# Batch 0 of a fused attention and mixer kernel: first loads in five pieces on one queue, casts on ScalarE, two buffer fills on GpSimd

## The chip, the cores and the metric

The kernel runs on one core of one Trainium2 chip. A core has a matrix engine (TensorE, PE in the profile; its weight loads are PEld), VectorE (DVE), ScalarE (ACT), GpSimd (POOL) and SyncE (SP), each with its own instruction queue that it works through in order, and 16 DMA engines. DMAs are issued from queues: SP and ACT have hardware queues (q1 and q10 in this profile), POOL has a software queue (q0). In this kernel the loads from POOL's queue turn float32 into bfloat16 on the way, the others do not.

The metric is the device time of one execution in microseconds (us). Four executions took 293.96 to 294.33 us, median 294.16 us. Times inside an execution are counted from the start of the profiled span.

## The reference

```python
B, H, S, D = 8, 8, 576, 64                      # q, k, v: [B, H, S, D] float32
scores = (q @ k.transpose(0, 1, 3, 2)) / sqrt(D)
scores = where(pos[:, None] // 64 >= pos[None, :] // 64, scores, -1e9)   # causal in blocks of 64
attn = softmax(scores)
x = (attn @ v).transpose(0, 2, 1, 3).reshape(B, S, 512)
xt = x.transpose(0, 2, 1)
h = relu(xt @ w_tok1) @ w_tok2                  # over the 576 tokens, 256 hidden
u = x + h.transpose(0, 2, 1)
out = u + relu(u @ w_ch1) @ w_ch2               # over the 512 channels, 1536 hidden
```

The row maximum is not subtracted in the kernel: it exponentiates the scores as they are and divides by the row sums.

## The kernel before

**Stages of a batch.** For each half of the heads ("hg", 0 or 1, four heads each) q and k are loaded, brought to bfloat16 and transposed in 32x32 blocks on DVE (line 440, tile `turned`). Scores are made transposed, keys on partitions and queries on columns (line 555, PSUM tiles `sc`). ACT exponentiates them into `e_sb` (line 574, 1024 columns at a time: 512 columns of two heads). DVE zeroes the 64x64 corners that the block mask excludes (line 580). PE multiplies by `vals`, which is v with a column of ones (line 602), so that the row sum comes out as the 65th column; DVE takes the reciprocal (line 624) and scales (line 630) into `x_sb`. Then come the token mixing (lines 788, 817, 832 and, from batch 1 on, 881), the channel products up (line 999) and down (line 1319, from batch 1 on 1228), and the output DMAs.

**Columns of e_sb.** Keys 0 to 511 are four blocks J of 128. The scores of a head are kept in 1536 columns, `ECOL[J]` being the first column of block J: 0, 576, 1024, 1344. `SETS` says which (column, first key, first query, width) regions are made together, 512 columns a set: set 0 is J = 0 and queries 0 to 511, set 1 the rest of J = 0 and J = 1, set 2 J = 2 and 3. `MASKS` gives the columns at which a set is masked: (0), (576), (1024, 1344). The last 64 keys go their own way, into `et_sb`, a part of the tile `vals` (lines 652 and 669).

**Batch 0** has its own form (`first_attention`, line 674). Its heads go in four pairs j; for each pair the sets are made in the order 2, 1, 0, so set 0 and its mask come last. The products with `vals` of a pair depend on all exps and masks of that pair.

**First loads (`load_qk`, line 404).** Only for batch 0 and hg 0, q and k are loaded in float32 by the hardware queues into `stage` (the tile `gT`), each in two halves of 9 of the 18 tokens that a partition holds: one half issued on SP and one on ACT (line 427). Each half is then cast (line 400; planned for ACT or DVE, all four were put on ACT), and each half transposed. Everything else is loaded by software DMAs from POOL: v of batch 0 (line 469, ten pieces), k and q of hg 1 (line 420), the token weights (line 488), the channel weights (lines 511, 520), and from batch 1 on q, k and v. POOL's queue also makes the identity matrix (`masks.py`) before its first load. The plan lets at most eight of its DMAs be outstanding.

**Fills (`init_tiles`, line 339).** DVE zeroes or sets paddings at the start (line 343): first `zeros`, from which PE runs, then parts of `turned`, `e_sb`, the weights and `vals`, among them the two buffers `et_sb` (128x640 bfloat16 each; 128x320 uint32 in the profile).

**Matmuls without use (`raise_clock`, line 366).** 16 products of `zeros` (line 372) and up to 110 smaller ones (line 379) keep PE running so that its clock is up. The latter are only put where the plan sees PE free, and only up to planned time 20; their results are not used.

**The order** of every queue comes from a planner in the file (class `Plan`). It knows for each piece of work its engines, a cost in us, its dependencies, a priority, a class `urgent`, and buffers that it takes and gives. It fills each engine in planned time (`run`), tries 1000 random changes of the priorities within +-4000 and keeps those that do not make the planned end later (`search`); the instructions are then emitted in planned order. Planned times are the planner's own, they are not measured. Of software DMAs it supposes that the first starts moving data at 6.2 (`soft` in line 115) and that they then follow one another; of hardware DMAs that they follow one another from 0.7 after the first issue (`hard`, `FIRST`); a DMA's data can be used 1.3 later.

Of the kernel before, what the change touches and what calls it, by code (L numbers as in the profile page):

```python
# [31 lines left out]
class Plan:  # L32
# [66 lines left out]
    def run(self):  # L99
# [12 lines left out]
        heapq.heapify(queued)  # L112

        avail = {e: [] for e in self.LAG}
        t, hard, soft, gives, order, mode = 0.0, 0.0, 6.2, [], [], 0
        left = len(self.ops)
        landed = [0.0] * 8

# [2 lines left out]
        while left:  # L121
# [13 lines left out]
            for e in ("PE", "ACT", "DVE", "POOL", "SP"):  # L135
                if busy[e] > t or e == "POOL" and landed[-8] > t:
                    continue
                for at, a in enumerate(avail[e]):
                    if self.fits(a[3]):
                        break  # L140
                else:
                    continue
                o = a[3]
                soon = t + 0.6 * o.cost[e]
                if any(
                    r < soon and self.ops[n].urgent > o.urgent and e in self.ops[n].engines
                    for r, n in queued
                ):
                    continue
                if any(  # L150
                    -u[0] > o.urgent and self.fits(u[3], [name for r, name, _ in gives if r < soon])
                    for u in avail[e][:at]
                ):
                    continue
                for x in o.engines:
                    del avail[x][bisect.bisect_left(avail[x], o.key)]
                left -= 1
                began = True
                for pools, note in o.take:
                    note["pool"] = next(p for p in pools if self.free[p])  # L160
                    note["slot"] = self.free[note["pool"]].pop(0)
                o.engine, o.start = e, t
                o.end = busy[e] = t + o.cost[e]
                if o.mode is None:
                    o.mode = mode
                if e == "PE" and o.mode != mode:
                    o.end = busy[e] = o.end + 0.1
                    mode = o.mode
                order.append(o)
                lag = self.LAG[e]  # L170
                if o.xfer is not None:
                    first = o.end + self.FIRST[e]
                    if e == "POOL":
                        soft = max(soft, hard, first) + o.xfer
                    else:
                        hard = max(hard, first) + o.xfer
                    o.end, lag = (soft if e == "POOL" else hard), 1.3
                    if e == "POOL":
                        landed.append(o.end + lag)
                for note in o.give:  # L180
                    heapq.heappush(gives, (o.end + lag * (not o.quick), note["pool"], note["slot"]))
                for u in o.users:
                    same = u.engines == (e,) and o.xfer is None
                    u.ready = max(u.ready, o.end + (0.05 if same else lag))
                    u.waiting -= 1
                    if not u.waiting:
                        heapq.heappush(queued, (u.ready, u.n))
# [8 lines left out]
def kernel(  # L196
# [133 lines left out]
    def act_cost(n):  # L330
        return 0.08 + n * 0.000833
# [7 lines left out]
    def init_tiles():  # L339
        def fill(engine, key, prio, *parts):  # L340
            for t, value in parts:
                def emit(o, t=t, value=value):
                    (nc.vector if engine == "DVE" else nc.gpsimd).memset(t, value)

                pads.setdefault(key, []).append(P.add(engine, 0.17, emit, (), prio))

        for i, t in enumerate(kT):
            fill("DVE", ("kT", i), -1e4 + i, (t[:, S:640, :], 0.0))
        for i in range(2):
            fill(  # L350
                "DVE", ("v", i), -60 + 20 * i,
                (v1[i][64:128, 4, :, :], 0.0),
                (v1[i][:, 0:4, :, 64:65], 1.0),
                (v1[i][0:64, 4, :, 64:65], 1.0),
            )
            fill("DVE", ("e", i), -70, (e_sb[i][:, :, 1536:1600], 0.0))
            fill("DVE", ("et", i), -70, (et_sb[i], 0.0))
        fill("DVE", "zeros", -1e5, (zeros, 0.0))
        fill("DVE", "w1", -70, (w1_sb[64:128, 4, :], 0.0), (w1o_sb[0:64, :], 0.0))

        def emit(o):
            make_identity(nc, ident)

        pads["ident"] = [P.add("POOL", 0.6, emit, (), -1e6)]
# [24 lines left out]
    def warm_up():  # L389
        def emit(o):  # L390
            nc.scalar.activation(warm, nc.const_aps.tensor(0.0, (128, 1), FP32), EXP)

        P.add("ACT", 1.5, emit, (), -9e3)


    EVAC = ("DVE", "ACT")
# [7 lines left out]
    def load_qk(b, hg, after=[]):  # L404
        i = (2 * b + hg) % 3
        first = b == 0 and hg == 0
        prio = 10 * b + 4 * hg - (100 if b == 0 else 0)
        parts = ((0, NB // 2), (NB // 2, NB))
        done = []
        for n, (src, raw, dst) in enumerate(((k, kraw[i], kT[i]), (q, qraw[i], qT[i]))):  # L410
            hbm = src[b, 4 * hg : 4 * hg + 4].rearrange("h (p k) d -> (h p) (k d)", p=32)
# [6 lines left out]
            if not first:  # L418
# [1 line left out]
                    nc.gpsimd.dma_start(out=raw2, in_=hbm)  # L420

                loads = [P.add("POOL", 0.55, emit_load, raw_war, prio + n, xfer=8 * 0.184)]
            for f, (k0, k1) in enumerate(parts):
                if first:
                    def emit_load(o, k0=k0, k1=k1, hbm=hbm, st=st):
                        queue = nc.sync if o.engine == "SP" else nc.scalar
                        queue.dma_start(out=st[:, D * k0 : D * k1], in_=hbm[:, D * k0 : D * k1])

                    ld = P.add(("SP", "ACT")[f % 2], 0.45, emit_load, (), -1e4 + n, xfer=(k1 - k0) * 0.1)

                    def emit_cast(o, k0=k0, k1=k1, raw2=raw2, st=st):
                        cast(o, raw2[:, D * k0 : D * k1], st[:, D * k0 : D * k1])

                    w = D * (k1 - k0)
                    ld = P.add(EVAC, {"ACT": act_cost(w), "DVE": dve_cost(w)}, emit_cast, [ld], -1e4 + 2 + n)
                    reads(("g", 0), ld)
                    loads = [ld]

# [133 lines left out]
    def exp(dst, n, op, note, prio, urgent=0, give=None):  # L572
        def emit(o):
            nc.scalar.activation(dst, sc[SC.index(note["pool"])][:, :, 0:n], EXP, scale=scale)  # L574

        return P.add("ACT", act_cost(2 * n), emit, [op], prio, give=give or [note], urgent=urgent)

    def mask(e, c, hs, deps, prio, urgent=0):
        def emit(o):
            nc.vector.memset(e[64:128, hs, c : c + 64], 0.0)  # L580

        return P.add("DVE", 0.17, emit, deps, prio, urgent=urgent)

    def head_out(b, head, deps, prio, tail, urgent=0):
        hg, h = divmod(head, 4)

        ei = hg if b == 0 else b % 2
        vt, xt, et, e = v1[b % 2], x_sb[b % 3], et_sb[ei], e_sb[hg]
        shift = 0 if b % 2 == 0 else -64
        bank = {}  # L590

        def emit(o, chunks):
            u = bank_of(bank)[:, 0:330].rearrange("p (i c) -> p i c", c=66)
            for I in chunks:
                for J in range(I + 1):
                    if J < 4:
                        c = ECOL[J] + 128 * (I - J) + (shift if I == 4 else 0)
                        w = e[:, h, c : c + 128]
                    else:
                        c = 64 + 128 * h + (64 * hg if b else 0) + shift  # L600
# [39 lines left out]

    TAIL = (512, 512, 64)
    MASKS = ((0,), (576,), (1024, 1344))

    def first_tail(hg, heads, deps, prio):

# [28 lines left out]
    def first_attention(ready, v_ready):  # L674
# [3 lines left out]
        for j in range(4):  # L678
# [4 lines left out]
            prio = -3000 + j  # L683
            exps = []
            for n, s in enumerate((2, 1, 0)):
                width = sum(w for _, _, _, w in SETS[s])
                parts = tuple((hg,) + r for r in SETS[s])
                dst = e[:, hs, 512 * s : 512 * s + width]
                if j == 0 and n == 0:

                    note = {}
# [18 lines left out]
                if n == (1 if j else 2):  # L710
                    tails = first_tail(hg, heads, [op] + ready[hg], prio + 0.1 * n + 0.05)
                exps += these
                for c in MASKS[s]:
                    exps.append(mask(e, c, hs, these, prio, urgent=1))
            for h in heads:
                deps = exps + v_ready[hg] + pad + pads["e", hg]
# [751 lines left out]
```

## Time and profile before

| what | us |
|---|---|
| median of 4 executions | 294.16 |
| the profiled execution | 294.33 |
| its span | 292.5 |
| PE busy | 286.0 (98%) |
| DVE busy | 235.9 (81%) |
| ACT busy | 166.7 (57%) |
| POOL busy | 62.0 (21%) |
| first scores (line 555) begin | 8.51 |
| first exp (line 574) begins | 9.18 |
| last exp of batch 0 ends | 21.28 |
| first scores of batch 1 begin | 26.76 |
| last matmul group's end | 288.66 |

The profiled execution is 294.33 us long, of which the span from the first to the last profiled instruction is 292.5; 1.8 us lie around it. It stands 0.17 us above the median. PE counts as busy also while it multiplies zeros and while a matmul waits in the pipeline, so its 98% is no measure of use in the first 20 us.

### The profile page before, as it was taken

What the parts mean: (1) busy time and instruction counts of PE and PEld (TensorE: products, weight loads), DVE (VectorE), ACT (ScalarE), POOL (GpSimd) and SP (SyncE); (2) the same over time, 40 slices, a digit from 0 to 9 for tenths busy, and PEclk for the clock granted to TensorE, in tenths of its full rate; (3) what the DMA queues carried; (4) which work ended last, traced back from release to release, by engine and by line L of the source; (5) the groups of instructions that cost most, each with busy time, mean ns of one, the idle gap of its engine ahead of it and who ended that gap; (6) DMA issues with size and microseconds to landing.
All of it is one profiled execution on the core that took longest, in us unless ns stands there. A gap on an engine that the chain in (4) does not pass through costs nothing.

```text
span 292.5 us, 7674 instructions
## 1 busy us (share of the span) xinstructions
PE 286.0 (98%) x3252; PEld 180.4 (62%) x3252; DVE 235.9 (81%) x512; ACT 166.7 (57%) x236; POOL 62.0 (21%) x96
## 2 busy tenths in 40 slices
PE   8899999999999999999999999999999999999994
PEld 4566445554558765455774657775446885566883
DVE  5566768988959979959997979668998968969993
ACT  4797864576777563786656796433477004867000
POOL 8776353810430170170032000000000000000000
PEclk9999999999999999999999999999999999999998
DMA  8999999992793299995329012042000912130054
GB/s 213 187 199 210 207 186 182 225 198 81 115 131 74 43 163 198 167 129 64 73 16 211 5 32 42 2 145 54 3 0 10 154 72 74 36 142 5 0 183 145
DMA packets 64403, 31.99 MB, mean 109 GB/s; under 512 B 53104, under 2 KB 55024, under 8 KB 64368
## 3 DMA queue, kind: packets, MB, share of 16 engines
q0 software_dynamic: 44320, 17.34, 50.3%
q1 hardware_dynamic: 19760, 13.57, 17.3%
q8 instruction: 25, 0.41, 0.6%
q10 hardware_dynamic: 288, 0.59, 0.5%
q14 instruction: 10, 0.08, 0.1%
HBM read 35.85 MB, written 9.44 MB: 155 GB/s over the span
## 4 chain that ended last, share of the span: by engine, by line
PE 90%; ACT 4%; DMA 2%; DVE 1%; issue 0%; ACTq 0%
PE mm L1228 18%; PE mm L999 15%; PE sc L555 9%; PE mm L602 9%; PE mm L1319 7%; PE mm L1104 6%; PE late L1104 6%; PE mm L788 6%; PE late L1228 4%; PE mm L881 4%; ACT e_sb L574 4%; PE mm L1026 3%; DMA gT<-in_q_dram 2%; DVE turned L440 1%; PE mm L912 1%; PE mm L962 0%
## 5 line engine op out<-in xcount | busy, mean ns | idle before, releaser
L574 ACT ACTIVATE e_sb<-sc 128x1024 bf16<-128x1024 f32 x95 | 92.5, 1030 | 32.9 <-PE sc L555 32.4
L999 PE MATMUL mm<-uT,wc_sb 128*128 128x512 bf16 x192 | 46.1, 382 | 0.0
L469 POOL DMA_DIRECT2D vals<-in_v_dram x45 | 36.9, 837 | 26.3 <-PE mm L602 22.4
L440 DVE STREAM_TRANSPOSE turned<-raws 128x288 int32<-128x288 int32 x64 | 40.0, 706 | 2.2 <-ACT raws L400 1.8
L555 PE MATMUL sc<-turned 32*128 32x64 bf16 (+4 forms) x744 | 35.4, 281 | 1.4 <-DVE turned L440 0.8
L602 PEld LDWEIGHTS <-e_sb 128*128 128x128 bf16 x896 | 31.3, 97 | 6.7 <-issue 3.2
L999 PEld LDWEIGHTS <-wc_sb 128*128 128x128 bf16 x192 | 20.0, 116 | 20.8 <-issue 5.7
L602 PE MATMUL mm<-vals,e_sb 128*128 128x65 bf16 x868 | 32.5, 193 | 0.0
L630 DVE TENSOR_TENSOR x_sb<-mm,rinv 128x320 bf16<-128x320 f32 x62 | 29.1, 485 | 1.3
L776 DVE TENSOR_SCALAR gT<-mm 128x512 bf16<-128x512 f32 x27 | 18.6, 689 | 11.8 <-PE mm L999 11.7
L1228 PEld LDWEIGHTS <-sums 128*128 128x128 bf16 x252 | 24.1, 98 | 4.4 <-issue 1.2
L1228 PEld LDWEIGHTS <-gT 128*128 128x128 bf16 x240 | 22.8, 98 | 4.5 <-issue 1.3
L555 PEld LDWEIGHTS <-turned 32*128 32x128 bf16 x752 | 12.8, 93 | 19.6 <-issue 17.3
L400 ACT COPY e_sb<-mm 128x512 f32<-128x512 f32 x14 | 8.2, 591 | 26.6 <-PE mm L1104 25.0
L774 ACT ACTIVATE gT<-mm 128x512 bf16<-128x512 f32 x24 | 14.3, 597 | 10.9 <-PE mm L999 10.8
L580 DVE MEMSET e_sb<- 64x128 uint32 (+1 forms) x72 | 10.6, 153 | 10.4 <-ACT e_sb L574 6.4
L788 PE MATMUL mm<-x_sb,w_sb 128*128 128x512 bf16 (+1 forms) x102 | 17.9, 316 | 0.0
L420 POOL DMA_DIRECT2D raws<-in_k_dram x15 | 8.2, 553 | 41.3 <-DVE turned L440 32.1
L896 DVE TENSOR_TENSOR u_sb<-mm,x_sb 128x512 bf16<-128x512 f32 x24 | 15.4, 684 | 1.4 <-PE mm L881 1.3
L1251 DVE TENSOR_TENSOR o_sb<-mm,u_sb 128x512 f32<-128x512 f32 x20 | 13.7, 687 | 3.4 <-PE mm L1228 2.6
L1228 PE MATMUL mm<-wd_sb,sums 128*128 128x256 bf16 x132 | 15.7, 273 | 0.0
L1251 DVE TENSOR_TENSOR o_sb<-mm,o_sb 128x512 f32<-128x512 f32 (+1 forms) x19 | 12.0, 632 | 4.4 <-PE mm L1228 4.2
(146 smaller groups left out, 457.9 us busy)
## 6 DMA issues: line engine op xcount, KB each, us to landing
out_dram<-o_sb SPq DMA_DIRECT2D x14, 512.0 KB, 3.1
raws<-in_k_dram POOLq DMA_DIRECT2D x15, 288.0 KB, 6.3
raws<-in_q_dram POOLq DMA_DIRECT2D x15, 288.0 KB, 7.1
vals<-in_v_dram POOLq DMA_DIRECT2D x28, 128.0 KB, 5.9
wc_sb<-in_moe_w_ch_dram POOLq DMA_DIRECT2D x8, 192.0 KB, 6.5
wc_sb<-in_moe_w_ch_dram POOLq DMA_DIRECT2D x3, 512.0 KB, 10.5
out_dram<-o_sb SPq DMA_DIRECT2D x10, 128.0 KB, 2.3
vals<-in_v_dram POOLq DMA_DIRECT2D x15, 64.0 KB, 5.4
```

The costliest lines, as they stand in the source:

```text
L440: nc.vector.transpose(dst[:, 0:S, :] .rearrange("p s e -> p (s e)") .bitcast(I32) .rearrange("p (a k) -> p k a", k=NB)[:, k0:k1], raw2.bit ...
L469: nc.gpsimd.dma_start(out=dst, in_=src)
L555: nc.tensor.matmul(out=home(n)[:, c0 : c0 + w], lhsT=kT[i][r, j0 : j0 + 128, par], rhs=qT[i][r, i0 : i0 + w, par], start=(par == 0), stop= ...
L574: nc.scalar.activation(dst, sc[SC.index(note["pool"])][:, :, 0:n], EXP, scale=scale)
L602: nc.tensor.matmul(out=u[:, I, 0:65], lhsT=w, rhs=vt[:, J, head, 0:65], start=(J == 0), stop=(J == I),)
L630: nc.vector.tensor_tensor(out=xt[:, :, 64 * head : 64 * head + 64], in0=u[:, :, 0:64], in1=ri.to_broadcast([128, 5, 64]), op=MULT,)
L788: nc.tensor.matmul(out=bank_of(bank)[:, w * n : w * n + w], lhsT=wt[:, tt : tt + 255 : 2], rhs=xt[:, c, cols], start=(c == 0), stop=(c == 4),)
L999: nc.tensor.matmul(out=bank_of(bank), lhsT=wc1_sb[:, m, channels(cc)], rhs=uT[b % 2][:, :, m, :], start=(m == 0), stop=(m == NDM - 1),)
L1104: nc.tensor.matmul(out=bank_of(bank), lhsT=x(m), rhs=y[:, :, m, :], start=first and m == 0, stop=m == 1, skip_group_check=not first,)
L1228: nc.tensor.matmul(out=bank_of(bank)[:, 256 * i : 256 * i + 256], lhsT=x[:, kk, 128 * i : 128 * i + 128], rhs=y[:, kk], start=first and i ...
L1251: nc.vector.tensor_tensor(out=dst, in0=src, in1=other, op=ADD)
L1319: nc.tensor.matmul(out=ps, lhsT=gt[:, cc, c0 : c0 + 128], rhs=wc2_sb[:, cc, cols], start=(cc == 0 and not turned), stop=(cc == NDC - 1),)
```

## The change

Seven edits, all for the start of the kernel or in the planner's figures:

- `load_qk`: the first k is loaded in two pieces and the first q in three (9, 5 and 4 of the 18 tokens of a partition), all five issued on SP; none on ACT. Casts are given to ACT alone, with the highest class of urgency. The transposes of q follow the three pieces.
- `init_tiles`: the two `et_sb` buffers are zeroed on POOL, with a priority just behind the identity matrix, so ahead of POOL's loads.
- `LAST_SETS`, `LAST_COLS`, `LAST_MASKS`, `ECOL_LAST`: for batch 0, hg 1, the columns of `e_sb` are laid out anew. J = 1 takes columns 0 to 447 and J = 0 columns 448 to 1023, so both corners to be masked (columns 0 and 448) are in set 1, and set 0, the last one made, has no mask.
- the table load on ACT (`warm_up`) gets a planned time from 0.75.
- planner figures: software DMAs start at 5.0 instead of 6.2; no 0.05 between two dependent pieces on PE; an exp costs 0.02 less; an urgent mask 0.12 instead of 0.17; a hardware load costs 0.42 of issue instead of 0.45, 0.089 a token instead of 0.1, and begins at 0.7.

Because the planner sees other numbers, the order of the instructions can differ anywhere in the program. The number of useful matmuls, of exps and of masks is the same.

```diff
-        t, hard, soft, gives, order, mode = 0.0, 0.0, 6.2, [], [], 0
+        t, hard, soft, gives, order, mode = 0.0, 0.0, 5.0, [], [], 0
...
-                    u.ready = max(u.ready, o.end + (0.05 if same else lag))
+                    u.ready = max(u.ready, o.end + ((e != "PE") * 0.05 if same else lag))
...
-            fill("DVE", ("et", i), -70, (et_sb[i], 0.0))
+            fill("POOL", ("et", i), -1e5, (et_sb[i], 0.0))
...
-        P.add("ACT", 1.5, emit, (), -9e3)
+        P.add("ACT", 1.5, emit, (), -9e3, at=0.75)
...
-        parts = ((0, NB // 2), (NB // 2, NB))
...
-            for f, (k0, k1) in enumerate(parts):
+            edges = (0, 9, 18) if not (first and n) else (0, 9, 14, 18)
+            for f, (k0, k1) in enumerate(zip(edges, edges[1:])):
                 if first:
                     def emit_load(o, k0=k0, k1=k1, hbm=hbm, st=st):
-                        queue = nc.sync if o.engine == "SP" else nc.scalar
-                        queue.dma_start(out=st[:, D * k0 : D * k1], in_=hbm[:, D * k0 : D * k1])
-
-                    ld = P.add(("SP", "ACT")[f % 2], 0.45, emit_load, (), -1e4 + n, xfer=(k1 - k0) * 0.1)
+                        nc.sync.dma_start(out=st[:, D * k0 : D * k1], in_=hbm[:, D * k0 : D * k1])
+
+                    ld = P.add("SP", 0.42, emit_load, (), -1e4 + n, xfer=0.089 * (k1 - k0), at=0.7)
...
-                    ld = P.add(EVAC, {"ACT": act_cost(w), "DVE": dve_cost(w)}, emit_cast, [ld], -1e4 + 2 + n)
+                    ld = P.add("ACT", act_cost(w), emit_cast, [ld], -1e4 + 2 + n, urgent=3)
...
-        return P.add("ACT", act_cost(2 * n), emit, [op], prio, give=give or [note], urgent=urgent)
+        return P.add("ACT", act_cost(2 * n) - 0.02, emit, [op], prio, give=give or [note], urgent=urgent)
...
-        return P.add("DVE", 0.17, emit, deps, prio, urgent=urgent)
+        return P.add("DVE", 0.12 if urgent else 0.17, emit, deps, prio, urgent=urgent)
...
+        ecol = ECOL_LAST if b == 0 and hg == 1 else ECOL
...
-                        c = ECOL[J] + 128 * (I - J) + (shift if I == 4 else 0)
+                        c = ecol[J] + 128 * (I - J) + (shift if I == 4 else 0)
...
+    ECOL_LAST = (448, 0, 1024, 1344)
+    LAST_SETS = (((0, 0, 64, 512),), ((0, 128, 128, 448), (448, 0, 0, 64)), SETS[2])
+    LAST_COLS, LAST_MASKS = (512, 0, 1024), ((), (0, 448), MASKS[2])
...
-                width = sum(w for _, _, _, w in SETS[s])
-                parts = tuple((hg,) + r for r in SETS[s])
-                dst = e[:, hs, 512 * s : 512 * s + width]
+                parts = tuple((hg,) + r for r in (SETS, LAST_SETS)[hg][s])
+                width, c0 = 512, (512 * s, LAST_COLS[s])[hg]
+                dst = e[:, hs, c0 : c0 + 512]
...
-                for c in MASKS[s]:
+                for c in (MASKS, LAST_MASKS)[hg][s]:
```

## The prediction

> **What bounds the kernel now.** I read first the chain of work that ended last, in order of time, from 0 to 28 us, then the timeline of PE and POOL over the first 9 us, then busy time by stretches, then the DMA issues. The chain (start, length, what):
>
> ```profile
> 1.18 5.26 DMA gT<-in_q_dram
> ...
> 6.46 0.68 ACT raws L400
> ...
> 7.17 1.30 DVE turned L440 x2
> ...
> 8.51 0.24 PE sc L555 x4
> ...
> 9.18 1.91 ACT e_sb L574 x2
> ...
> 17.38 1.84 ACT e_sb L574 x2
> ...
> 19.27 0.63 PE sc L555 x4
> 19.89 1.01 PE mm L602 x30
> 20.91 1.12 PE mm L788 x20
> ```
>
> The first scores wait for the second half of q, issued on ACT: landed at 1.18 + 5.26 = 6.44, two casts, two transposes, 8.51. From 9.18 the chain is ACT's exps, back to back to about 21.28; from 19.27 on it is PE, to 288.66. The stretches (from, to, length, then busy us of PE, PEld, DVE, ACT, POOL) say the same:
>
> ```profile
> 8.50:13.20 4.70, 4.60 (x62) 2.63 (x61) 2.71 (x8) 4.02 (x7) 3.82 (x6) 1.00 1.64 180
> 13.20:19.27 6.07, 5.83 (x114) 3.96 (x109) 3.57 (x16) 6.07 (x12) 4.88 (x10) 1.00 1.50 194
> 19.27:26.70 7.43, 7.39 (x128) 5.84 (x128) 5.26 (x16) 5.28 (x12) 3.56 (x8) 1.00 1.15 208
> 26.70:60.00 33.30, 33.24 (x370) 17.01 (x373) 24.57 (x54) 22.31 (x29) 18.88 (x27) 1.00 1.53 199
> ```
>
> ACT is full from 13.20 to 19.27; PE is full from 19.27, with 0.04 us idle up to 26.70 and 0.06 up to 60. Of PE's busy time from 8.50 to 19.27, 2.54 us are the dummies of line 379, so PE has room there and none later. What starts the exps sooner therefore moves everything behind it by as much, as long as loads keep up. DMA is the danger: its share is above 1 up to 60.
>
> **The first scores.** Three things must be there: the data, DVE's transposes, and PE. The timeline (start, length, engine, what, idle before):
>
> ```profile
> 1.19 5.11 PE L372 MATMUL mm<-wd_sb 128*128 128x512 bf16 x16 [1.19 <-DVE wd_sb L343]
> 6.14 1.58 PE L379 MATMUL mm<-wd_sb 128*128 128x256 bf16 x13
> 8.51 0.24 PE L555 MATMUL sc<-turned 32*128 32x64 bf16 x4 [0.79 <-DVE turned L440]
> 0.24 0.10 POOL L1452 MEMSET const-float32-0.0<- 128x1 f32 x1 [0.24 <-issue]
> 0.74 0.20 POOL masks.py:197 MEMSET ident<- 128x128 bf16 x1 [0.29 <-POOLq L1452]
> ```
>
> *Data.* The four halves are 4 x 288 KB = 1.18 MB; packets begin at 1.75. Over 2.0 to 4.5 both hardware queues together moved 0.89 MB (356 GB/s), q1 alone 0.50 MB of it (200 GB/s). What one queue does alone the start does not show. The stores do: 512 KB take 3.1 us from issue to landing, 256 KB 2.1, so 262 GB/s. Ends: at 356 GB/s the last piece is moved at 1.75 + 3.3 = 5.05, at 262 at 6.25, at 200 at 7.65; landing comes some 0.5 later (q10's last packets stand in the stretch 5.5 to 6.0, its landing is 6.44). Landed: 5.55, 6.75, 8.15. I take 5.55 to 6.75, since the 200 is a share taken beside another queue. The five issues of about 0.42 end at 0.74 + 5 x 0.42 = 2.84 and are ahead of the data.
>
> The Trainium skill, "DMA: Bandwidth & Descriptors", section "Issuing engines are not separate DMA queues", says that issues from several engines end on the same 16 DMA engines and save only the sequencer's time. By it the one queue would lose nothing and the last landing would be 5.55; by the share that q1 had here it would be 8.15. No run here settles it yet.
>
> *Cast and transposes.* After the last landing there remain a cast of 256 columns and a transpose of 4 of 18 tokens. Nearest rows: ACT 0.38 for 128x256 (line 774, from PSUM) against 0.67 for the 576-column cast; transpose 0.70 for 9 of 18, so 0.31 by size. I take 0.38 + 0.40 + 0.07 of gaps = 0.85, against 2.07 before (6.44 to 8.51). The pieces ahead (casts 0.58 apart, transposes 0.57) end by 6.4 if q's first piece lands by 4.8. So DVE is ready between 6.8 and 7.6. The casts were all on ACT already, so that part of the edit costs nothing, and ACT has only its table load (1.67 to 2.95) to do till then.
>
> *PE.* Here is the limit that the change does not move. PE's queue has 16 + 13 dummies ahead of the scores, and they end at 6.14 + 1.58 = 7.72. Their number comes from the plan (a count of instructions, not a time of the chip): dummies start at planned 6.11, every 0.11, until the scores are due. Before, the last q is due at 6.05, cast to 6.61, +0.2, transpose 0.55, +0.18: 7.54, last dummy before 7.47, so 13, as the trace has it. After: pieces land at 1.82 + 0.089 x 36 + 1.3 = 6.32 for the last; q's casts end at 6.08, 6.43, 6.72; +0.2, transposes to 6.84, 7.15, 7.41; +0.18 = 7.59, last dummy before 7.52: 13 again. Scores start at about 7.75: **-0.76**. Ends: 7.1 with five dummies fewer (-1.4), 9.0 at 200 GB/s (+0.5). If data come later than 6.9, PE's cover is gone and each us is one.
>
> **The exps.** Their number and size stay; the smaller planned costs (exp, mask, gap on PE, table load, software start) are numbers in the planner and cost nothing by themselves. 12 us of ACT work just move.
>
> **The last mask of hg 1.** Now the product waits for the mask: last exp ends 21.28, DVE's memset at 21.57 takes 0.11, products at 22.03. Removing it is worth between 0 (PE was busy till then with lines 788 and 817) and 0.7 (21.28 to 22.03). PE's 0.04 us of idle is the nearer row: **-0.2**. The columns' new places change no sizes.
>
> **The fills on POOL.** DVE loses two of 0.33 (1.98 to 2.65), where nothing waits: worth 0. POOL's memset took 0.10 for 1 element and 0.20 for 128, so 0.0081 per ten: 640 bfloat16 are 0.62, 320 uint32 would be 0.36, strict proportion to the 0.20 gives 1.03. Two of them: 0.72, 1.24 or 2.06; I take 1.24, since the row is bfloat16. The skill ("VectorE: DVE Perf Modes", "Zero memsets can be issued as uint32 (trn2)") speaks against the move: it gives a memset one cycle per element, and the halving by uint32 for a Vector-engine memset. If POOL had the halving too, the delay would be 0.72, and the sum 0.15 less.
>
> All of POOL's loads queue behind: v, k and q of hg 1, weights, batch 1. Up to 0.4 comes back, as software packets meet fewer hardware ones at 4.9 to 5.9. What is late next, by landings in the DMA view (issue + time to landing): q of hg 1 at 3.47 + 6.2 = 9.67 with transposes at 11.31 for scores at 15.37, cover 2.8 to spare; q of batch 1 hg 0 at 16.14 + 7.1 = 23.24 for scores at 26.76 less 1.3 of transposes, cover 2.2, less 0.96 for the earlier schedule: 1.2, just used up, cost 0, beyond it us for us. Tightest is v of hg 1: last piece 12.59 + 5.4 = 17.99, used by products at 19.82, now 18.86: cover 0.87, so 1.24 is 0.37 late and 0.84 is not. The products wait on PE with the last scores and ACT's exps behind them. Cost 0 to 0.37, taken **+0.15**.
>
> **Sum.** -0.76 - 0.2 + 0.15 = -0.81. Profiled execution 294.33 - 0.81 = 293.52; it lies 0.17 above the median, so **293.35** for the median. The search over priorities runs anew: PE idles 0.4 us between 8.50 and 60 outside dummies, so a new order can gain little there and lose some tenths; that is 0 +- 0.4.
>
> **Rivals.**
> 1. *More: the whole 1.4.* Fewer dummies ahead of the scores, and batch 1's scores, no longer planned behind loads supposed 1.2 later than now, fill the gaps up to 26.7: -1.4 - 0.4 = 292.4. For it: DVE ready by 6.8 at 356 GB/s. Against: the count of 13.
> 2. *Hidden: no change.* One queue feeds at 220 to 240 GB/s, last landing at 7.2 to 7.6, scores at 8.05 to 8.45, so -0.1 to -0.5 and the +0.15: 293.85 to 294.2. For it: q1's 200 beside q10. Against: the stores' 262. That the loads do not run at once is the change not doing what it says.
> 3. *Slower: POOL's fills hold up its loads.* If they wait until DVE's own fills end (4.09), the first v load goes out at 4.1 instead of 1.44, and with their own 1.24 at 5.3: delay 2.65 to 3.9. Place: v of hg 1, 20.6 to 21.9 against 18.86, so 1.8 to 3.0 late, -0.96 beside it: +0.8 to +2.0, 295.0 to 296.2. It is slower than before from a delay of 1.83, by more than 0.6 us from 2.4. Against: the identity's memset and its next step ran beside DVE's fills at 0.86 to 1.31 without a stretch.
>
> **Chances.** Forecast 0.50 (293.0 to 293.6), rival 1 0.13, rival 2 0.20, rival 3 0.17. A measurement of this kernel tells about 0.2% (0.6 us) from no change. The forecast case reaches to 293.57 mostly: 0.46 faster, 0.04 same; rival 1 all faster; rival 2 all same. Faster 0.59, same 0.24, slower 0.17. Range: 292.4 (rival 1's time) to 294.8 (the point at which POOL's delay is 2.4, worth +0.6); beyond are most of rival 3 and the edge of rival 1, under 2 in 10.
>
> **What would show it.** After: 13 dummies of line 379 ahead of the scores, these at 7.7 to 7.8 with PE itself, not DVE, ending the wait; last q landing between 5.5 and 6.8; two memsets of `vals` on POOL of 0.62 each, the first v load near 2.7; last exp near 20.5; products of hg 1 at or just after v's landing at 18.8 to 19.2; batch 1's scores near 25.9. The forecast is wrong if the scores wait for DVE past 8, if POOL's memsets take over 1 us each, or if PE idles more than a few tenths between 20 and 60.

## The result, and the profile after

The changed kernel takes 294.91 us (median of 35 executions, 294.09 to 296.83), the kernel before 294.30 beside it (57 executions, 293.96 to 294.95). The ratio is 1.0027, with an interval of 1.0019 to 1.0034: slower by 0.27%, where 293.35 was forecast. Five of the changed kernel's executions (295.79 to 296.83 us) ran at a granted TensorE clock of 0.987 to 0.994, all others of both kernels at 0.997 or more; without those five its mean is 294.95 instead of 295.14, against 294.36 before, still 0.20% slower. The profiled execution after is 295.31 us, its span 293.5, and lies 0.40 above its median; the one before was 294.33 and 292.5.

The timeline of ACT after, over its casts of the first loads (start, length, engine, what, idle before), shows when the pieces have landed, since ACT waits for them:

```profile
3.77 1.38 ACT L400 CAST raws<-gT 128x576 bf16<-128x576 f32 x2 [1.54 <-DMA gT<-in_k_dram]
6.37 0.67 ACT L400 CAST raws<-gT 128x576 bf16<-128x576 f32 x1 [1.23 <-DMA gT<-in_q_dram]
8.17 0.46 ACT L400 CAST raws<-gT 128x320 bf16<-128x320 f32 x1 [1.12 <-DMA gT<-in_q_dram]
9.25 0.40 ACT L400 CAST raws<-gT 128x256 bf16<-128x256 f32 x1 [0.62 <-DMA gT<-in_q_dram]
10.82 1.94 ACT L573 ACTIVATE e_sb<-sc 128x1024 bf16<-128x1024 f32 x2 [1.17 <-PE sc L554]
```

The first half of k is there at 3.75, sooner than before (4.55). Then the pieces of q come 1.8 and 1.1 apart; the last lands at 9.22, where before it was 6.44. The timeline of PE after:

```profile
1.19 6.13 PE L372 MATMUL mm<-wd_sb 128*128 128x512 bf16 x16 [1.19 <-DVE wd_sb L343]
7.16 1.58 PE L379 MATMUL mm<-wd_sb 128*128 128x256 bf16 x13
10.15 0.32 PE L554 MATMUL sc<-turned 32*128 32x320 bf16 x2 [1.42 <-DVE turned L439]
```

13 dummies stand ahead of the scores, but they end at 8.74, and PE then waits 1.42 for DVE's transposes. The timeline of POOL:

```profile
1.25 1.20 POOL L343 MEMSET vals<- 128x640 bf16 x2
2.40 0.69 POOL L419 DMA_DIRECT2D raws<-in_k_dram  x1
3.08 3.60 POOL L468 DMA_DIRECT2D vals<-in_v_dram  x5
6.63 0.60 POOL L419 DMA_DIRECT2D raws<-in_q_dram  x1
```

Two fills, and the first load goes out at 2.40 instead of 1.44. It is not the same load any more: the new plan puts k of hg 1 first (it was v), and q of hg 1 behind five v loads, 3.2 later than before.

Busy time by stretches (PE, PEld, DVE, ACT, POOL), the same ones as before:

```profile
8.50:13.20 4.70, 3.20 (x50) 1.74 (x47) 2.52 (x8) 2.91 (x6) 3.88 (x7) 1.00 1.40 158
13.20:19.27 6.07, 6.07 (x101) 3.88 (x99) 3.60 (x16) 6.07 (x14) 4.47 (x8) 1.00 1.39 174
19.27:26.70 7.43, 7.43 (x145) 5.83 (x142) 5.72 (x20) 5.39 (x10) 4.58 (x9) 1.00 1.17 208
26.70:60.00 33.30, 33.23 (x369) 17.10 (x367) 22.78 (x51) 24.61 (x34) 18.59 (x26) 1.00 1.41 204
```

Only the first stretch lost: PE 4.60 to 3.20, ACT 4.02 to 2.91. From 13.20 on ACT is full as before, from 19.27 on PE is. So the loss is one shift, and it can be followed point by point: first scores 8.51 to 10.15 (+1.64), first exp 9.18 to 10.82 (+1.64), last exp of batch 0 21.28 to 22.92 (+1.64), first channel product of batch 0 27.33 to 28.47 (+1.14: the last mask and the new order give 0.50 back), span +1.0.

The chain of work that ended last in this kernel does not pass through the first loads, though. From the two fills (1.30 to 2.40) it stays on POOL's queue and its loads, up to a load of v that is issued at 31.96 and lands at 43.77, just as PE needs it. From 28 to 60 PE is busy for 31.93 of 32.00 us, so the two lines of work end nearly together: a sooner start of the scores alone would meet the late loads.

### The profile page after: what moved, and what is told of

The parts are those of the page before. It is cut to its first block, busy times and chain, and to the rows that moved or that the text cites. A ratio compares the mean times of both kernels' runs of the same rounds, so it can differ in the third digit from the quotient of the medians.

```text
span 293.5 us, 7704 instructions
## 1 busy us (share of the span) xinstructions
PE 286.9 (98%) x3250; PEld 180.2 (61%) x3250; DVE 230.0 (78%) x502; ACT 171.5 (58%) x246; POOL 63.1 (21%) x98
## 4 chain that ended last, share of the span: by engine, by line
PE 83%; DMA 11%; POOL 3%; issue 1%; ACT 0%; DVE 0%; POOLq 0%
PE mm L1231 20%; PE mm L1002 11%; PE mm L602 8%; PE sc L554 8%; PE mm L1107 6%; DMA vals<-in_v_dram 6%; PE late L1107 6%; PE mm L1322 6%; PE mm L791 4%; PE mm L1029 4%; PE mm L884 4%; DMA raws<-in_q_dram 3%; DMA raws<-in_k_dram 2%; PE late L1231 2%; POOL vals L468 1%; PE late L1322 1%
## 5 line engine op out<-in xcount | busy, mean ns | idle before, releaser
L439 DVE STREAM_TRANSPOSE turned<-raws 128x288 int32<-128x288 int32 (+1 forms) x65 | 40.3, 697 | 8.0 <-PE sc L554 3.9
L602 PE MATMUL mm<-vals,e_sb 128*128 128x65 bf16 x840 | 31.5, 193 | 0.1
L777 ACT ACTIVATE gT<-mm 128x512 bf16<-128x512 f32 x35 | 20.9, 598 | 8.4 <-PE mm L1002 7.7
L779 DVE TENSOR_SCALAR gT<-mm 128x512 bf16<-128x512 f32 x16 | 11.0, 689 | 12.8 <-PE mm L1002 12.7
L1254 DVE TENSOR_TENSOR o_sb<-mm,u_sb 128x512 f32<-128x512 f32 x23 | 15.8, 687 | 5.5 <-PE mm L1231 5.5
L777 ACT ACTIVATE gmT<-mm 128x512 bf16<-128x512 f32 x11 | 6.4, 597 | 19.7 <-PE mm L1029 19.7
L1231 PE MATMUL mm<-wd_sb,sums 128*128 128x256 bf16 x144 | 17.7, 273 | 0.0
L899 DVE TENSOR_TENSOR u_sb<-mm,x_sb 128x512 bf16<-128x512 f32 x22 | 13.9, 681 | 3.1 <-PE mm L884 3.0
L791 PE MATMUL mm<-x_sb,w_sb 128*128 128x512 bf16 (+1 forms) x94 | 16.0, 311 | 0.0
L1107 PEld LDWEIGHTS <-raws 128*128 128x128 bf16 x96 | 9.3, 98 | 9.9
```

The costliest lines, as they stand in the source:

```text
L439: nc.vector.transpose(dst[:, 0:S, :] .rearrange("p s e -> p (s e)") .bitcast(I32) .rearrange("p (a k) -> p k a", k=NB)[:, k0:k1], raw2.bit ...
L602: nc.tensor.matmul(out=u[:, I, 0:65], lhsT=w, rhs=vt[:, J, head, 0:65], start=(J == 0), stop=(J == I),)
L777: nc.scalar.activation(dst, src, RELU)
L791: nc.tensor.matmul(out=bank_of(bank)[:, w * n : w * n + w], lhsT=wt[:, tt : tt + 255 : 2], rhs=xt[:, c, cols], start=(c == 0), stop=(c == 4),)
L1107: nc.tensor.matmul(out=bank_of(bank), lhsT=x(m), rhs=y[:, :, m, :], start=first and m == 0, stop=m == 1, skip_group_check=not first,)
L1231: nc.tensor.matmul(out=bank_of(bank)[:, 256 * i : 256 * i + 256], lhsT=x[:, kk, 128 * i : 128 * i + 128], rhs=y[:, kk], start=first and i ...
```

## The experiments

In each experiment the planned order is the one of the kernel that it starts from; only what its diff shows is changed. None leaves out part of the computation; the 4 dummies that one of them drops are products of zeros that nobody uses. The table has all of them. Landings, scores and products are from one profiled execution each; "rest" is from batch 0's first channel product to the end of the last matmul. The ratio is taken against executions of the kernel before that were made beside the kernel in question (not all on the same chip), so it is not the quotient of two medians of this table; where rows are compared, the ratio counts.

| kernel | median us | ratio to before, 95% | last first load lands | first scores | q of batch 1 lands | first channel product | rest |
|---|---|---|---|---|---|---|---|
| before | 294.30 | 1 | 6.44 | 8.51 | 23.26 | 27.33 | 261.3 |
| after | 294.91 | 1.0027 (1.0019 to 1.0034) | 9.22 | 10.15 | 25.87 | 28.47 | 261.4 |
| after, two queues | 294.97 | 1.0017 (1.0002 to 1.0031) | 7.36 | 8.29 | 26.08 | 27.98 | 261.2 |
| after, v first | 294.89 | 1.0013 (1.0003 to 1.0023) | 6.70 | 8.42 | 25.39 | 27.77 | 261.2 |
| after, fills on DVE | 296.31 | 1.0063 (1.0046 to 1.0079) | 9.96 | 10.89 | 27.09 | 29.21 | 261.2 |
| after, four pieces | 295.55 | 1.0048 (1.0023 to 1.0073) | 8.07 | 9.36 | 25.97 | 27.88 | 261.9 |
| before, one queue | 295.05 | 1.0029 (1.0019 to 1.0039) | 7.70 | 9.20 | 25.63 | 28.02 | 261.3 |
| before, fills on POOL | 294.25 | 1.0000 (0.9990 to 1.0011) | 6.32 | 8.72 | 25.99 | 27.89 | 261.3 |
| two queues, fills on DVE | 294.36 | 0.9996 (0.9982 to 1.0010) | 7.81 | 8.73 | 25.63 | 27.53 | 261.2 |
| one queue, old loads | 295.80 | 1.0046 (1.0033 to 1.0060) | 6.52 | 8.00 | 25.97 | 27.87 | 262.8 |
| two queues, old loads | 295.86 | 1.0050 (1.0033 to 1.0068) | 6.38 | 8.86 | 25.91 | 27.81 | 262.4 |
| two queues, old loads, fills on DVE | 293.76 | 0.9974 (0.9962 to 0.9985) | 6.36 | 8.18 | 23.75 | 26.51 | 261.5 |
| the same, one queue | 294.96 | 1.0015 (1.0001 to 1.0029) | 7.61 | 9.06 | 24.38 | 27.39 | 261.5 |
| the same, two queues, 4 dummies fewer | 293.45 | 0.9977 (0.9962 to 0.9992) | 6.14 | 7.86 | 23.35 | 26.19 | 261.3 |

The column "rest" is the first reading. Apart from three kernels it is 261.2 to 261.5: what the edits cost in the other kernels, they cost before 28 us.

In the expectations, the theories whose letter is A lay the loss to the first loads alone. E, formed after the first four, says that two bounds stand one behind the other: the first loads from the hardware queue, and POOL's loads.

### Two queues again

```diff
-                        nc.sync.dma_start(out=st[:, D * k0 : D * k1], in_=hbm[:, D * k0 : D * k1])
+                        queue = nc.scalar if f % 2 else nc.sync
+                        queue.dma_start(out=st[:, D * k0 : D * k1], in_=hbm[:, D * k0 : D * k1])
```

The second piece of k and of q is issued on ACT, ahead of its table load.

> The changed kernel with its order of instructions kept; only the second piece of k and of q is issued on ACT, ahead of its table load, instead of SP. Theory A (the single hardware queue loses its share of the DMA engines as soon as software packets come, from 4.6 us on): two queues get two turns in three, the last piece of q lands at 6.0 to 7.2 instead of 9.22, the first scores start at 7.8 to 8.2 instead of 10.15, and the time falls by 1 to 1.7 us, to 293.2 to 293.9. Rival B (the first loads are late because software packets are ahead of them, however many queues there are): last landing stays above 8.5, time 294.6 to 295. Rival C (the new order of the whole program costs the time, the start is made up for later): the scores come sooner and the time stays at 294.6 to 295.

The last piece lands at 7.36 and the scores begin at 8.29, 1.86 sooner, right behind the dummies and the transposes, which end at nearly the same time. The time is 294.97, by the ratio 0.10% below after and not clear of noise. That is the outcome of rival C; the chain of waits of this kernel (start, length, what) names a load instead:

```profile
19.17 6.91 DMA raws<-in_q_dram
26.08 0.02 issue
26.10 0.04 DVE turned L446
26.14 0.53 issue
26.66 0.70 DVE turned L446
27.37 0.04 issue
27.41 0.64 PE sc L561 x16
```

q of batch 1 was issued on POOL at 19.17 and landed at 26.08; it is transposed to 27.37, and batch 1's scores wait for it. Ahead of these lines the chain is on POOL's queue, back to the fills; k of hg 1, for example, is issued at 2.40 and lands at 8.76. PE was busy for 6.98 of the 8.00 us from 20 to 28, against 7.90 in the kernel before. In the kernel before, this q was issued at 16.14 and landed at 23.26.

### v first

```diff
+    def MOVE():
+        return [(TAG["qk", 0, 1, 0], TAG["v", 0, 0, 4])]
...
+        for op, ref in MOVE():
+            order.remove(op)
+            order.insert(order.index(ref) + 1, op)
```

On POOL, k of hg 1 goes behind the five v loads instead of ahead of them.

> The changed kernel with its order kept, except that on POOL the load of k of hg 1 (packets of 2304 bytes, 191 ns each) comes after the five v loads of hg 0 (128 bytes, 32 ns), as it stood behind v loads before. Theory A1 (turns are taken by packet, so long software packets take the most from q's short ones): between 4.6 and 6.5 the hardware queue keeps most of the time, last landing 6.5 to 7.8 instead of 9.22, time 293.8 to 294.5. Rival (many small packets crowd it just as much, as between 6.5 and 8.9 in the changed kernel, where up to 537 software packets ran in half a us): landing 8.5 to 9.5, time 294.7 to 295.1.

The one queue lands its last piece at 6.70 now, as the first theory said, and DVE is done at 7.74; the scores start at 8.42, since the dummies end only then (8.49 by their modelled ends). The time hardly moves: 294.89, by the ratio 0.14% below after, not clear of noise and far from the 293.9 to 294.5 of that theory. What binds next in this kernel is q of hg 1 (its chain of waits):

```profile
6.61 6.32 DMA raws<-in_q_dram
12.94 0.02 issue
12.96 1.26 DVE turned L445 x2
```

Before, that q was issued at 3.47 and had landed by 9.64. With its transposes ending at 14.22 ACT is no longer full from 13 to 20 (6.09 of 7.00).

### Fills back on DVE, and q in two pieces

```diff
-                    (nc.vector if engine == "DVE" else nc.gpsimd).memset(t, value)
+                    nc.vector.memset(t, value)
```

> The changed kernel with its order kept, except that the two fills of et_sb run on DVE again; POOL's first load goes out 1.14 us earlier, near 1.26. Theory A: software packets come at 3.5 instead of 4.6 and meet more of the first loads; last landing of q 9.5 to 10.5, scores 10.5 to 11.5, time 295.2 to 296. Rival D (the fills' delay of all software loads is what costs): last landing about the same, software loads 1.1 earlier, time 294.0 to 294.5.

POOL's loads start 0.96 sooner, at 1.44, and the time is 1.4 us worse, 296.31. The last piece lands at 9.96, q's first piece at 7.84 instead of 6.35. Here are the DMA views of three kernels from 4.5 to 6.5 (packets, MB, time of the packets as a share of 16 engines; q0 is POOL's queue, q1 is SP's). After:

```profile
q0 software_dynamic: 89, 0.20, 58.0%
q1 hardware_dynamic: 238, 0.30, 47.0%
```

After, with the fills on DVE:

```profile
q0 software_dynamic: 107, 0.19, 73.1%
q1 hardware_dynamic: 67, 0.08, 16.2%
```

After, with v first:

```profile
q0 software_dynamic: 1069, 0.13, 105.1%
q1 hardware_dynamic: 315, 0.35, 53.7%
```

Where k of hg 1 is first, POOL's packets average 1.8 to 2.2 KB (0.20 MB in 89, 0.19 in 107), where v is first 120 bytes. SP's queue gets 0.08 MB when the large packets come from about 4.4 (fills on DVE), 0.30 when they come in numbers from 4.8 (after), and 0.35 beside the small ones, which come from 5.0. So these views mix the size of POOL's packets with the time of their coming. What is left of the first loads at 5.5 is 0.32 MB, 0.16 and 0.06. From then on little goes through beside small packets either. From 6.5 to 9.0 in the kernel after, where v packets have come too:

```profile
q0 software_dynamic: 2033, 0.35, 178.7%
q1 hardware_dynamic: 97, 0.09, 11.2%
```

In 2.5 us the last 0.09 MB of q got through: 36 GB/s, where from 2.0 to 4.5, with nothing beside it, the same queue moved 0.77 MB, 306 GB/s. The fills on POOL delayed the rival packets and so protected the first loads, the reverse of what the forecast charged them for.

```diff
-                        nc.sync.dma_start(out=st[:, D * k0 : D * k1], in_=hbm[:, D * k0 : D * k1])
+                        if k0 == 14:
+                            return
+                        last = 18 if k0 == 9 else k1
+                        nc.sync.dma_start(out=st[:, D * k0 : D * last], in_=hbm[:, D * k0 : D * last])
```

The second and third piece of q go out as one DMA; casts and transposes stay as they are.

> The changed kernel with its order kept, except that the second and third piece of q are one DMA of 9 tokens (packets of 2304 bytes instead of 1280 and 1024); casts and transposes stay in three pieces. Theory A2 (one packet a turn, so halving the packet halves what q gets a turn): 128 packets less to be served in turns, last landing 7.3 to 8.4 instead of 9.22, time 294.1 to 294.7. Rival (the share is one of time or bytes, not of packets): landing 9 to 9.5, time 294.8 to 295.2.

It lands at 8.07, as theory A2 said, where in the kernel after the second piece alone had landed at 8.14: between these two traces, cutting q's second half into two loads costs 1.15 at the landing. The scores start 0.79 sooner. The time, 294.42 to 297.54, is not proven different from after, and misses the 294.1 to 294.7 of that theory; an earlier start alone again brought nothing.

### Two queues and POOL's loads at once

The forecast had assumed that POOL's loads keep their order. In the next four, POOL's first 26 loads are put into the order of the kernel before ("old loads"), with and without the other two edits.

```diff
         order = P.search(1000)
+        like_before(order)
```

Two queues with fills on DVE, the new order of loads:

> As the run with the first loads on two queues (all else and the order as in the changed kernel), and the two et_sb fills back on DVE, so that POOL's loads start 1.1 us earlier. Theory E (two bounds lie one behind the other: the first scores, and the software load of batch 1's q, which landed at 26.08 with two queues against 23.26 before): q of batch 1 lands near 25.0, the first scores stay below 8.8, the channel products of batch 0 begin at 27.2 to 27.5 instead of 27.98, time 294.2 to 294.6. Rival C (the new order of the compute engines alone costs it): they begin at 27.8 to 28.1 again, time 294.8 to 295.2.

One queue, fills on POOL, old loads:

> The changed kernel, with POOL's first 26 loads put into the order in which the kernel before has them (two v loads, k and q of hg 1, ..., k and q of batch 1 before the fourth of the second channel weights' pieces); one queue, fills on POOL, compute order as in the changed kernel. Theory E: q of hg 1 lands near 10.8 instead of 12.53 and q of batch 1 near 24.3 instead of 25.87; the first scores come at 8.4 to 9.6, since v goes first; channel products of batch 0 begin at 27.0 to 27.8, time 293.9 to 294.6. Rival C: they begin no earlier than the scores make it, 27.9 or more, time 294.7 to 295.1.

Two queues, fills on POOL, old loads:

> As the last, with the first loads on two queues. Theory E: both bounds are gone; first scores 7.8 to 8.3, q of batch 1 near 24.2, channel products of batch 0 from 26.4 to 27.0, time 293.3 to 293.9, faster than the kernel before. Rival C: 27.3 or later, time 294.2 or more.

Two queues, fills on DVE, old loads:

> As the last, with the et_sb fills on DVE: of the edits of the first 10 us only the pieces, the casts' places and the order of the compute engines are left. Theory E: software loads 0.7 to 1.1 earlier, which are no bound any more, time within 0.3 us of the run with two queues and the old order of loads, 293.3 to 294.0. If the fills' delay still bound something, it would be 0.4 to 1 us faster than that run.

Undoing two things, queue and fills, gives 294.36, the time of before, as theory E said, and rival C falls with it. Undoing all three gives 293.76, and that beats both kernels (0.9974, 0.9962 to 0.9985). What is left of the change in it is the casts, the three pieces of q, the new place of the masks and the new order of computation. Its stretches and its first PE lines:

```profile
13.20:19.27 6.07, 6.07 (x117) 4.22 (x118) 3.29 (x18) 6.07 (x12) 5.08 (x10) 1.00 1.50 187
19.27:26.70 7.43, 7.38 (x134) 5.42 (x133) 5.52 (x16) 5.20 (x10) 3.49 (x7) 1.00 1.14 202
26.70:60.00 33.30, 32.88 (x357) 16.96 (x361) 23.70 (x53) 23.58 (x32) 18.55 (x26) 1.00 1.41 204
```

```profile
1.19 5.63 PE L390 MATMUL mm<-wd_sb 128*128 128x512 bf16 x16 [1.19 <-DVE wd_sb L361]
6.66 1.58 PE L397 MATMUL mm<-wd_sb 128*128 128x256 bf16 x13
8.18 0.31 PE L574 MATMUL sc<-turned 32*128 32x320 bf16 x2
```

The scores follow the dummies without a wait.

The two kernels with old loads and fills on POOL are 2 us slower than it, and neither theory had that. Their first loads are fine (6.52 and 6.38), but the rest grew to 262.8 and 262.4. (In the one with two queues the scores begin 0.68 late as well, at 8.86, since the dummies end at 8.92; in the one with one queue they begin at 8.00, and it loses as much.) The waits of PE from 8 to 60 in the one with two queues (us in total, times, longest):

```profile
PE mm L622 <- DMA vals<-in_v_dram: 0.7, 2, 0.6
PE sc L574 <- DVE turned L459: 0.5, 1, 0.5
```

and of DVE from 20 to 60:

```profile
DVE turned L459 <- DMA raws<-in_k_dram: 2.4, 2, 1.8
```

With the fills on DVE only the first of these waits is left on PE, at 0.2. So the fills' delay of 0.96 at POOL's first load is 2.16 at q of batch 1 (23.75 to 25.91) and 2.0 at k of its hg 1 (29.31 to 31.35), and PE is busy for 31.05 of the 32.00 us from 28 to 60, against 31.58.

### Each step in the order of before

```diff
-                        queue = nc.sync if o.engine == "SP" else nc.scalar
+                        queue = nc.sync
```

The kernel before with its four halves on SP.

> The kernel before with its order kept; only the two halves issued on ACT go to SP's queue as well. Theory E: four pieces of 2304 bytes a packet, and v's 128-byte packets from 4.9 us: last landing 6.3 to 7.3 (6.44 before), first scores 8.4 to 9.2, and since q of batch 1 lands unchanged near 23.3, with 2.2 us to spare, the time moves by -0.1 to +0.7, to 294.2 to 295.0. If the single queue alone were the cost of the change, it would be at least +0.6, 294.9 or more.

295.05, as much as the whole change. The last half lands at 7.70 instead of 6.44, the scores begin 0.69 later and the last matmul ends 0.68 later. So the single queue alone can cost as much as the change, which theory E had not expected; q of batch 1 is not waited for, though it lands at 25.63 and not near 23.3.

```diff
-                    (nc.vector if engine == "DVE" else nc.gpsimd).memset(t, value)
+                    (nc.gpsimd if key[0] == "et" else nc.vector).memset(t, value)
```

The kernel before with the two fills on POOL, behind the identity and ahead of its loads.

> The kernel before with its order kept; only the two et_sb fills run on POOL, ahead of its loads. Theory E (a late start of POOL's loads grows on its way: 0.96 us became 2.16 at q of batch 1 between the two runs with two queues and the old loads): first v load at 2.4 instead of 1.44, q of batch 1 at 25.0 to 25.6 instead of 23.26, batch 0's channel products at 27.8 to 28.8 instead of 27.33, time 294.8 to 295.8. The rival, as I predicted it: the delay stays 1.1 at most and is covered but for 0.15, time 294.2 to 294.5.

294.25, a ratio of 1.0000 (0.9990 to 1.0011). POOL's loads are late here too (q of batch 1 at 25.99, k of its hg 1 at 31.23), and yet PE is busy for 32.00 of 32.00 us from 28 to 60: there the order of before has slack that the order of after, with the old loads, lacks. Earlier it is not so clear. The profiled execution, at 294.82 well above its median, does wait for that q, with batch 1's scores at 27.32 instead of 26.76; that the median shows no cost says only that this is not the rule.

### From the fastest, one step each

All five pieces on SP in the fastest kernel:

> The fastest run so far with the five first pieces on SP's queue alone. Software packets (v, 128 bytes) come near 4.9, when one queue still has some 0.25 MB in pieces of 1280 and 1024 bytes a packet to move. Theory A/E: last landing 6.8 to 8.5 instead of 6.36, scores 8.5 to 10, nothing of it hidden by late software loads now: time 294.1 to 295.3. Rival (the queue does not matter when v goes first, as the scores at 8.00 in the run with one queue and the old order suggest): scores 8.0 to 8.4, time 293.6 to 294.0.

294.96, some 0.4% more than 293.76 (1.0015 against 0.9974). The last piece lands at 7.61 instead of 6.36; DVE is ready at about 8.5, and PE's dummies, ending at 9.1 in this execution, hold the scores to 9.06:

```profile
1.19 6.51 PE L390 MATMUL mm<-wd_sb 128*128 128x512 bf16 x16 [1.19 <-DVE wd_sb L361]
7.54 1.58 PE L397 MATMUL mm<-wd_sb 128*128 128x256 bf16 x13
```

So its profiled scores don't show by themselves how much the queue costs; the times do. Last, since the dummies bind in the fastest kernel, four fewer of them:

```diff
-            for _ in range(WARM):
+            for _ in range(WARM - 4):
```

> The fastest run so far (two queues, old order of loads, fills on DVE, 293.76) with 12 instead of 16 of the first products of zeros, so that PE's dummies end some 0.9 to 1.4 us earlier. Theory F (the dummies, which ended at 8.24 there, hold the first scores; DVE was done near 7.7): scores at 7.6 to 7.8 instead of 8.18, time 293.1 to 293.5. Rival: DVE or a lower clock holds them, scores at 8.0 or more or slower exps behind, time 293.6 to 294.0.

```profile
1.19 5.30 PE L390 MATMUL mm<-wd_sb 128*128 128x512 bf16 x12 [1.19 <-DVE wd_sb L361]
7.86 0.31 PE L574 MATMUL sc<-turned 32*128 32x320 bf16 x2
```

The scores begin 0.32 sooner; the dummies end at 7.93 and still hold them, since the 12 products took 5.30 where the 16 took 5.63, and DVE was done at 7.56. The ratio, 0.9977 (0.9962 to 0.9992), is no different from 0.9974. Inconclusive.

### What each step is worth

From the fastest kernel, one step alone, by the ratios: one queue +0.4% (1.0015), the new order of POOL's loads +0.2% (0.9996, its interval just touching that of the fastest), fills on POOL +0.8% (1.0050). All three together, which is the change, cost 0.5% (1.0027), less than their sum: the new order of loads gets along with late loads better than the old one (0.9996 without and 1.0017 with the fills, against 0.9974 and 1.0050), and the fills hold back the packets that starve the one queue. With the fills on POOL the one queue costs nothing that can be told from noise, +0.10% with the new loads and -0.04% with the old ones; with the fills on DVE it costs 0.67% and 0.41%. All eight combinations of the three were run, so the sums are measured; the reasons given for them rest on one trace of each kernel.

## Why the prediction was wrong

**The step that failed is "Data"**, in the first scores: "Landed: 5.55, 6.75, 8.15. I take 5.55 to 6.75, since the 200 is a share taken beside another queue." The last piece landed at 9.22, beyond even the far end. The share beside another queue was the nearer row, for another queue is still there: not ACT's, but POOL's, whose packets come from about 4.6 on. The rates of a queue by itself were right where they held (306 GB/s from 2.0 to 4.5, between 262 and 356), and the kernel with one queue and old loads landed at 6.52, inside the range taken. What was missing is that the last third of the five pieces would still be on the way when POOL's packets came (0.35 MB passed after 4.6). The step behind it was right: from the landing to the scores it took 0.93, and 0.85 was counted. In the profiled executions the sum's -0.76 for the first scores became +1.64.

**The order of POOL's loads was taken as unchanged.** The text gave the new plan +-0.4 for PE's order and never asked which load would then go first. The plan put k of hg 1 there, and that is the one with the large packets. Moving it alone brings the landing from 9.22 to 6.70. The new order of the loads also made q of hg 1 late (12.53, before 9.64).

**One bound was followed, and there were three.** "As long as loads keep up" stood in the text, but the covers were worked out for POOL's old order, at the fills' delay only. By measurement q of batch 1 landed 2.6 later than before, not 1.24, and v of hg 1, which was called the tightest, at 20.48 instead of 17.96, 2.5 later (with only the fills moved it lands at 18.80). Once the first loads are mended, q of batch 1 or of hg 1 decides, which is why two queues alone and v first alone bring next to nothing. So the wrong landing accounts for the late start, but not for the time by itself.

**The dummies.** 13 of line 379 ahead of the scores, as counted. But they ended at 8.74 instead of 7.72, since the 16 products before them took 6.13 instead of 5.11. Even with the data at 6.75 the scores of that execution would not have begun before 8.74, 0.23 later than before, so the -0.76 hung on a length that differed from one profile to the next. With v first, where the data were there in time, it is the dummies that held the scores to 8.42.

**The fills.** Sized right: 0.62 each was forecast and the profile has 0.63 each, two between 1.25 and 2.45; a halving did not show on POOL. The first load was late by 0.96, not 1.24. The cost of +0.15 (0.05%) lies within the interval in the order of before (0.00%, up to 0.11%), for which its covers were worked out. In the new order of computation, planned for loads 1.2 sooner and run with loads 0.96 later, the cover is gone: +0.76% from the fastest kernel with the old loads, +0.21% with the new ones. In the change itself they help more than they harm (296.31 without them).

**The last mask.** -0.2 was forecast. From the last exp to the first channel product it took 6.05 before, 5.55 after and 5.56 in the fastest kernel: -0.5, which holds the rest of the new order too. Casts and planner figures showed no cost by themselves (the fastest kernel has them); that a planner's figure moves loads was the part that was not free.

**The rivals.** "Hidden" had the right place and not enough of it: 220 to 240 GB/s for the one queue, where 36 were left in the end. "Slower" had the right sign by the wrong mechanism: POOL's fills ran at once, beside DVE's, and its loads went out at 2.40.

The Trainium skill, "DMA: Bandwidth & Descriptors", section "Issuing engines are not separate DMA queues", says that issuing from several engines saves the sequencer's time and no more. Here that depends on the software traffic beside it. With the fills on DVE it doesn't hold: one queue in place of two cost 0.29% in the order of before, with the landing at 7.70 instead of 6.44, and 0.4% in the fastest kernel, with 7.61 instead of 6.36. With the fills on POOL and the old loads it does: 6.52 against 6.38, and the same time (1.0046 and 1.0050). The sequencer's time alone is not the difference, since the last issue goes out 0.95 us later on one queue in all three pairs. By itself, one queue did reach 306 GB/s, against 356 for two in the kernel before.

## What to carry to other kernels

Before loads are put onto one queue, look at what else will be moving when the last of them is on the way: a queue's rate by itself says nothing about its share beside the packets of another one. When a planner's figures are changed, compare which load goes first and where the cover of each later load is, since an order planned for earlier loads can have less slack for late ones (with the old loads, the fills cost the new order 0.8% and the order of before nothing). And when undoing one part changes nothing, undo it together with the next one: a bound can hide behind another.

## What the hardware showed unexpectedly

- With one hardware queue and POOL's queue active, neither the size nor the number of POOL's packets alone gave the share. From 5.5 to 6.0, with loads still to move in each, SP's queue moved 0.04 MB beside 35 packets of POOL with 0.08 MB in all (after), 0.01 MB beside 25 with 0.06 MB (after, fills on DVE), 0.05 MB beside 397 with 0.05 MB (after, v first) and 0.13 MB beside 142 with 0.02 MB (before, one queue).
- POOL's packets did not simply follow its first issue. From 4.0 to 4.6 there were 8, 28 and 105 of them in the three kernels with one queue and the fills on DVE, at most 1 in the four with one queue and the fills on POOL, and none with two queues, wherever the fills were.
- The 16 first products took 5.11 us (before), 6.13 (after), 5.63, 5.88, 6.18 and 6.51 in other kernels, though nothing stands ahead of them on PE. They start 0.43 us apart at first and 0.22 apart after a step that came between 4.2 us (before) and 7.0 us (the kernel with 6.51), while the granted clock reads 1.00 throughout. Whether it varies by execution or by kernel was not tried; each kernel was profiled once. It puts up to 1.4 us between the dummies' ends, and it is a candidate, no more, for the part of after's spread that its clock does not go with.
